# Gate sums moved to TensorE identity products, and the last low-part pass of two feed-forward slices issued as a row pair behind attention scores

## Chip, cores and metric

One Trainium2 chip, one core. The metric is device microseconds of one execution of the program; the time given is the median of several runs.

## The reference

Two parts in a row. The first is a recurrent attention (mLSTM) over 4 batches, 8 heads, 768 steps, head size 40:

```
m_new  = max(f[t] + m, i[t]);  f_stab = exp(f[t] + m - m_new);  i_stab = exp(i[t] - m_new)
C      = f_stab * C + i_stab * outer(v[t], k[t]);   n = f_stab * n + i_stab * k[t]
y[t]   = sigmoid(o[t]) * (C @ q[t]) / max(|n . q[t]|, 1)
```

The second is a feed-forward layer on the 3072 resulting rows of 320: `h = x @ w_in` (320 to 2048), `g = h * clip(h + 3, 0, 6) / 6`, `out = g @ w_out` (2048 to 320). All inputs and the output are float32.

## The kernel before

**Attention.** The time axis is cut into 6 chunks of 128 steps in each batch, so there are 24 chunks. Eight *units* of three chunks each are worked off in order; each unit has two *tasks*, one for each quad of four heads. For each task and chunk there is: `gate` (builds the 128x128 decay weights `gw` of four heads: from the chunk's cumulated log gates, by TensorE for the first seven, by a DMA broadcast `gw<-gsc` and a mask on GpSimd for the others, then four exponentials on ScalarE), `front` (state product L611, four score products q.k in pairs of 64-row halves L694, four products with the carried state L697, then VectorE multiplies scores by weights, L702, and from unit 2 on splits the result into three bfloat16 parts `p`), and `back` (weights times values, L742 or L744 to L747). `fin` normalises, applies the output gate, transposes (L799) and splits the result into `xh` and `xl`, the high and low float32r parts of the feed-forward's input. A front waits until the front before it has made its `p`.

**Gates.** `gates(c0, n)` works off `n` chunks of the gate sequences as [32, 128 n] tiles; `GP = [1, 2, 1, 2]` says how the six chunks are grouped. VectorE scans the running maximum `m_s`, forms the stabilised log forget gate `lf` and its cumulated sum `g_s` by chunk; GpSimd and VectorE form `i_s - m_s - g_s` (L458, L477); TensorE transposes that and `g_s` (L488, L490) into one PSUM bank; VectorE copies both out (`cT`, `gTs`; L492, L496), a product with `last` (L503) broadcasts the chunk's final sum, VectorE adds it to `cT` (L505), and ScalarE makes the exponentials `eG`, `wT` and `dec`.

**Feed-forward.** For each unit the 2048 hidden columns are 16 *slices* of 128. `mm1(u, f)` makes one slice of `h` for 384 rows: eight passes of 384 columns into one of two PSUM banks (`mm`): three for each of the two full 128-row blocks of the input (high.high, high.low, low.high), and two for the last 64 input rows. For those, `wtl` holds the high part of the weights in one half of the partitions and the low part in the other (the halves swap between even and odd slices), and the x tile holds its rows twice. So the seventh pass gives high.high plus low.high, and the eighth high.low plus low.low. Then ScalarE (L907) and VectorE (L909) make `g`, which frees the bank, and ScalarE and VectorE split it (L404, L917). `mm2(u, p)` takes a pair of slices: three row tiles, six products of 320 columns each (L936 to L938), accumulated over the unit in three further banks. Six `g` slots exist. `evac` copies the sums out and stores them.

**Order.** The order on every engine is made when the program is built, by a list planner (`Plan`): each step is a job with a due time and a list of events that it needs; the planner keeps a clock for each engine and picks the next request by readiness and due time. The program then runs in that order; an engine works its queue in order and waits for semaphores. The due times come from constants (`T0`, `SPAN` for a unit's place, `AH` for how far attention runs ahead, `MV` for the feed-forward, `BKO` for `back`, `FIN0` for the first unit's `fin`, `G0` to `G2` for gates, `STICK` for staying with attention). `ENGINES` gives for each kind of elementwise step the engine or the choice of engines. While TensorE has nothing to do before the feed-forward opens, `warm` puts 128-column products `pw` (L425) on it.

Of the kernel before, what the change touches and what calls it, by code (L numbers as in the profile page):

```python
# [46 lines left out]
SPAN = 70.624  # L47
T0 = 123.535
AH = 19.252
GP = [1, 2, 1, 2]  # L50
G0 = -120.578
G1 = -25.639
G2 = 24.583
AH1 = 73.471
FC = 0
FCS = {2: [[(0, 2)], [(0, 1), (1, 1)]], 3: [[(0, 3)], [(0, 2), (2, 1)], [(0, 1), (1, 1), (2, 1)], [(0, 1), (1, 2)]], 1: [[(0, 1)], [(0, 1)]]}
LON = -2.289
WAI = 24.113
WAO = -0.73
WAS = 84.596  # L60
MV = -25.163
DELTA = -1.445
EGW = 1
EV = 127.005
EG = 30.396
# [7 lines left out]
RATE = 3689.588  # L73
WN = 128
DELTA0 = 0.131
# [4 lines left out]
BL = 7.052  # L80
T_WARM = 6.9
WGAP = 0.055
ENGINES = 'dxpxadzddadddxddxxdaaaaxdapx'
BG = 1.587
BA = -0.13
BD = -0.329
GS = 6
FD = 2
FIN0 = -97.197
# [58 lines left out]
class Plan:  # L148
# [4 lines left out]
    def __init__(self, slots):  # L153
        self.free = {e: 0.5 for e in "padgq"}
        self.dma = 0.5
        self.slots = {k: [(At({}), i) for i in range(n)] for k, n in slots.items()}
        self.done = {}
        self.jobs = []
        self.waiting = {}
        self.fresh = []  # L160
        self.left = 0
        self.work = {}
        self.recent = []
        self.port = 0.0
        self.last = ""
        self.n = 0

    def add(self, due, gen, after=(), att=1, slack=None, hot=False):
        self.n += 1
        j = dict(due=due, n=self.n, gen=gen, t=At({}), eng=None, req=None, after=list(after), need=set(after), att=att, slack=DELTA if slack is None else slack, first=slack is not None, hot=hot)  # L170
# [91 lines left out]
    def run(self):  # L262
        self.settle()
        while self.jobs:
            best = {}
            for j in self.jobs:
# [20 lines left out]
                if e == "p" and self.last != "moe" and j["gen"].__name__ not in ("mm1", "mm2", "warm"):  # L287
                    due -= STICK
                k = (late, start if late else 0.0, due, j["n"])
# [8 lines left out]
            else:  # L298
                end = start + cost
                if e == "p":  # L300
                    kind = {"mm1": "moe", "mm2": "moe"}.get(j["gen"].__name__, j["gen"].__name__)
# [45 lines left out]
def mlstm_moe_kernel(ctx: ExitStack, tc: tile.TileContext, ig, fg, qkd, natd, ond, w_in, w_out, ident_d, out):  # L347
# [66 lines left out]
    def warm():  # L414
# [13 lines left out]
        f_s=[BH, S], i_s=[BH, S], m_s=[BH, S], lf=[BH, S], g_s=[128, S], last=[128, 128], gTs=[128, NC, BH], one=[BH, L], sel=[128, 8, L]).items()}  # L428
# [7 lines left out]
    def gates(c0, n):  # L436
        f_s, i_s, m_s, lf, g_s, last, gTs, mask, one = (GT[k] for k in ("f_s", "i_s", "m_s", "lf", "g_s", "last", "gTs", "mask", "one"))
# [16 lines left out]
        yield "d", ld(w)  # L454
        nc.vector.tensor_tensor_scan(m_s[:, a:z], f_s[:, a:z], i_s[:, a:z], m_s[:, a - 1 : a] if c0 else NEG, ALU.add, ALU.max)
        b, t = max(a, 1), plan.now["t"]
        e = yield psub(26, w)
        E(e).tensor_sub(i_s[:, a:z], i_s[:, a:z], m_s[:, a:z])  # L458
        ti, plan.now["t"] = plan.now["t"], t
# [4 lines left out]
        for c in cs:  # L464
            ks = slice(c * L, c * L + L)
            yield "d", ld(L)
# [8 lines left out]
        plan.now["t"] = later(t, ti)  # L475
        yield "d", ld(w)
        nc.vector.tensor_sub(i_s[:, a:z], i_s[:, a:z], g_s[:BH, a:z])  # L477
        yield "wait", "ident"
        if c0 == 0 and GB:
            yield "a", ca(128)  # L480
            nc.scalar.copy(GT["identb"], ident)
            event("identb")
        gs = yield ("get",) + banks(0, "o")
        pb = bank(gs, [128, 4, 4, BH], f"pc{c0}")
        pc, pg, pl = (pb[:, k, :n] for k in range(3))
        yield "p", mat(2 * n, 128, 1, 32, 32)
        for c in cs:
            nc.tensor.transpose(pc[:, c - c0, :], i_s[:, c * L : (c + 1) * L], ident[:BH, :BH])  # L488
        for c in cs:
            nc.tensor.transpose(pg[:, c - c0, :], g_s[:BH, c * L : (c + 1) * L], ident[:BH, :BH])  # L490
# [4 lines left out]
        yield "d", cd(32 * n)  # L495
        nc.vector.tensor_copy(gTs[:, hs], pg)  # L496
        yield "a", ca(32 * n)
        nc.scalar.activation(eG[:, hs], pg, AF.Exp)
        if c0 == 0:
            yield "d", cd(128)  # L500
            nc.vector.tensor_copy(last, ident[:, 127:128].broadcast_to([128, 128]))
        yield "p", mat(2, 32 * n, 2)
        nc.tensor.matmul(pl, last, gTs[:, hs], start=True, stop=True)  # L503
        yield "d", cd(32 * n)
        nc.vector.tensor_tensor(wT[:, hs], pl, cT[:, hs], ALU.add)  # L505
        yield "a", ca(32 * n)
        nc.scalar.activation(wT[:, hs], wT[:, hs], AF.Exp)
# [56 lines left out]
    def weigh(task):  # L564
# [4 lines left out]
        for cp in range(UNITS[task // 2]):  # L569
            _, _, _, c, r0 = where(task, cp)  # L570
            if c < NC - 1:
                yield "wait", f"wT{c}"
                e = yield pick(6, d=ld(168), g=cg(168), a=4 * ca(42))
# [99 lines left out]
    def front(task, cp):  # L673
# [21 lines left out]
        if cur is not None:  # L695
            for z, j, rows, hs in halves:
                nc.tensor.matmul(sp[:, z, 2 * L + j * E2 : 2 * L + j * E2 + E2], st[rows, 0, hs], cur[rows, j, :], start=True, stop=True)  # L697
        put(*sg)
# [115 lines left out]
    def weight_slice(kind, i, n):  # L814
# [22 lines left out]
        if kind == "i":  # L837
# [6 lines left out]
            e = yield pick(4, a=0.44, d=Lock(0.63))  # L844
# [33 lines left out]
    A = {}  # L878

    def mm1(u, f):  # L880
# [10 lines left out]
        yield "p", mat(8, NT)  # L891
        for n, (w, x) in enumerate(seq):
            nc.tensor.matmul(hp, w, x, start=n == 0, stop=n == len(seq) - 1)  # L893
        event(f"m1_{u}_{f}")
# [81 lines left out]
    for task in range(2 * NU):  # L976
# [18 lines left out]
        for cp in range(n):  # L995
# [15 lines left out]
            plan.add(due(u, k + cp), front(task, cp), [f"st{nm}", *last, *old] + ahead(rank[task, cp]), 1, sl)  # L1011
# [90 lines left out]
```

## Time and profile before

| | |
|---|---|
| median of 3 runs (lowest, highest) | 492.16 us (492.15, 494.31) |
| the profiled execution: time, span in the trace | 493.0 us, 491.3 us |
| TensorE busy / VectorE / ScalarE / GpSimd | 484.1 / 392.5 / 268.5 / 34.1 us |
| granted TensorE clock | 1.00 |
| first feed-forward product | 44.16 us after the span's start |

The busy time of TensorE counts records that overlap (a record's end is modelled), so a rate is read from the distance between two starts. "PEld" is the loading of weights, "x8" is the number of instructions in a row of a timeline; a float32 product is two instructions, a float32r or bfloat16 product one. A window's row gives, for each engine, the busy time and the number of instructions.

### The profile page before, as it was taken

What the parts mean: (1) busy time and instruction counts of PE and PEld (TensorE: products, weight loads), DVE (VectorE), ACT (ScalarE), POOL (GpSimd) and SP (SyncE); (2) the same over time, 40 slices, a digit from 0 to 9 for tenths busy, and PEclk for the clock granted to TensorE, in tenths of its full rate; (3) what the DMA queues carried; (4) which work ended last, traced back from release to release, by engine and by line L of the source; (5) the groups of instructions that cost most, each with busy time, mean ns of one, the idle gap of its engine ahead of it and who ended that gap; (6) DMA issues with size and microseconds to landing.
All of it is one profiled execution on the core that took longest, in us unless ns stands there. A gap on an engine that the chain in (4) does not pass through costs nothing.

```text
span 491.3 us, 10775 instructions
## 1 busy us (share of the span) xinstructions
PE 484.1 (99%) x4227; PEld 463.7 (94%) x4227; DVE 392.5 (80%) x926; ACT 268.5 (55%) x618; POOL 34.1 (7%) x55
## 2 busy tenths in 40 slices
PE   8999999999999999999999999999999999999997
PEld 8999898999999999999999999999999999999997
DVE  7999999988878898879799887889698798533332
ACT  4967969846344654556355644555355443434333
POOL 5001101001000101010010100010000100000000
PEclk9999999999999999999999999999999999999999
DMA  7678776323231514143142333242221210001001
GB/s 269 216 272 244 254 228 204 111 82 109 65 108 46 183 55 118 55 126 115 43 126 86 107 106 106 71 120 83 67 84 63 85 41 2 0 2 40 1 1 40
DMA packets 24626, 50.79 MB, mean 103 GB/s; under 512 B 2560, under 2 KB 9024, under 8 KB 24576
## 3 DMA queue, kind: packets, MB, share of 16 engines
q1 hardware_dynamic: 24576, 50.11, 31.7%
q8 instruction: 33, 0.54, 0.5%
q14 instruction: 17, 0.14, 0.1%
HBM read 46.07 MB, written 4.03 MB: 102 GB/s over the span
## 4 chain that ended last, share of the span: by engine, by line
PE 85%; DVE 6%; DMA 4%; ACT 2%; issue 1%; SPq 1%; POOL 0%; POOLq 0%; DVEq 0%; ACTq 0%
PE h L893 33%; PE acc L936 11%; PE acc L938 10%; PE acc L937 10%; PE s L694 5%; PE s L697 3%; PE s L611 2%; DMA nat<-in_nat_dram 2%; DMA gw<-gsc 2%; PE x L799 1%; PE pw L425 1%; PE o L744 1%; PE o L742 1%; PE o L746 1%; DMA st<-in_qk_dram 1%; PE gb L655 1%
## 5 line engine op out<-in xcount | busy, mean ns | idle before, releaser
L907 ACT ACTIVATE g<-h,half 128x384 f32<-128x384 f32 x128 | 73.6, 576 | 97.8 <-PE h L893 97.5
L936 PE MATMUL acc<-vh,gh 128*128 128x320 f32 x384 | 122.1, 318 | 0.0
L938 PE MATMUL acc<-vh,gl 128*128 128x320 f32 x384 | 118.9, 310 | 0.0
L937 PE MATMUL acc<-vl,gh 128*128 128x320 f32 x384 | 118.8, 309 | 0.0
L909 DVE SCALAR_TENSOR_TENSOR g<-g,h 128x384 f32<-128x384 f32 x128 | 70.3, 550 | 44.9 <-ACT g L907 44.6
L893 PE MATMUL h<-xh,whi 128*128 128x384 f32 x256 | 91.0, 355 | 2.3 <-DVE g L909 2.2
L404 ACT CAST gh<-g 128x384 fp32r<-128x384 f32 x128 | 65.2, 511 | 47.8 <-DVE g L909 47.3
L893 PE MATMUL h<-xh,wlo 128*128 128x384 f32 x256 | 86.6, 338 | 0.0
L893 PE MATMUL h<-xl,whi 128*128 128x384 f32 x256 | 86.4, 338 | 0.0
L917 DVE TENSOR_TENSOR gl<-g,gh 128x384 fp32r<-128x384 f32 x128 | 73.9, 579 | 9.6 <-ACT gh L404 8.0
L936 PEld LDWEIGHTS acc<-vh,gh 128*128 128x128 f32 x384 | 72.1, 188 | 1.3
L937 PEld LDWEIGHTS acc<-vl,gh 128*128 128x128 f32 x384 | 72.2, 188 | 0.0
L938 PEld LDWEIGHTS acc<-vh,gl 128*128 128x128 f32 x384 | 72.1, 188 | 0.0
L667 ACT ACTIVATE gw<-gw,cT 128x128 f32<-128x128 f32 x164 | 54.2, 392 | 29.7 <-POOL gw L661 29.4
L893 PEld LDWEIGHTS h<-xh,whi 128*128 128x128 f32 x256 | 48.0, 188 | 6.2 <-DVE g L909 5.0
L661 POOL TENSOR_SCALAR_AFFINE_SELECT gw<-gw 128x512 f32<-128x512 f32 x41 | 27.9, 680 | 352.6 <-DMA gw<-gsc 208.4
L893 PEld LDWEIGHTS h<-xl,whi 128*128 128x128 f32 x256 | 48.2, 188 | 0.0
L893 PEld LDWEIGHTS h<-xh,wlo 128*128 128x128 f32 x256 | 48.1, 188 | 0.0
L893 PE MATMUL h<-xh,wtl 128*128 128x384 f32 x128 | 43.3, 338 | 0.0
L893 PE MATMUL h<-xl,wtl 128*128 128x384 f32 x128 | 43.2, 337 | 0.0
L702 DVE TENSOR_TENSOR gw<-s,gw 128x512 f32<-128x512 f32 x48 | 32.9, 685 | 6.3 <-PE s L697 5.3
L694 PE MATMUL s<-st 64*128 64x128 f32 x384 | 34.3, 297 | 0.3 <-DMA st<-in_qk_dram 0.3
(105 smaller groups left out, 754.2 us busy)
## 6 DMA issues: line engine op xcount, KB each, us to landing
st<-in_qk_dram SPq DMA_DIRECT2D x48, 256.0 KB, 3.1
gw<-gsc SPq DMA_DIRECT2D x41, 256.0 KB, 3.2
nat<-in_nat_dram SPq DMA_DIRECT2D x16, 492.0 KB, 4.4
rawi<-in_w_in_dram SPq DMA_DIRECT2D x8, 640.0 KB, 4.7
rawo<-in_w_out_dram SPq DMA_DIRECT2D x8, 640.0 KB, 4.9
on<-in_on_dram SPq DMA_DIRECT2D x8, 480.0 KB, 3.8
out_dram<-ob SPq DMA_DIRECT2D x24, 160.0 KB, 1.8
f_s<-in_fg_dram SPq DMA_DIRECT2D x1, 96.0 KB, 2.1
```

Of the source, the lines that this page charges most:

```text
L404: nc.scalar.copy(dst, src)
L661: nc.gpsimd.affine_select(gw, gw, pattern=[[0, 4], [1, L]], compare_op=ALU.is_ge, fill=NEG, base=0, channel_multiplier=-1)
L667: nc.scalar.activation(gw[:, h, :], src[:, h, :], AF.Exp, bias=cT[:, c, r0 + h : r0 + h + 1], scale=1.0)
L694: nc.tensor.matmul(sp[:, z, hs], st[rows, 1, hs], st[rows, 0, hs], start=True, stop=True)
L702: nc.vector.tensor_tensor(gw.rearrange("p (z j) l -> p z (j l)", z=2), sp[:, :, : 2 * L], gw.rearrange("p (z j) l -> p z (j l)", z=2), ALU ...
L893: nc.tensor.matmul(hp, w, x, start=n == 0, stop=n == len(seq) - 1)
L907: nc.scalar.activation(g, hp, AF.Relu, bias=half, scale=1.0 / 6.0)
L909: nc.vector.scalar_tensor_tensor(g, g, 1.0, hp, ALU.min, ALU.mult)
L917: E(e).tensor_sub(gl, g, gh.bitcast(F32))
L936: nc.tensor.matmul(acc, gh[:, ts_], VH[f // 4][:, f % 4, :], start=f == 0, stop=False)
L937: nc.tensor.matmul(acc, gh[:, ts_], VL[p][:, f % 2, :], start=False, stop=False)
L938: nc.tensor.matmul(acc, gl[:, ts_], VH[f // 4][:, f % 4, :], start=False, stop=f == NF - 1)
```

## The change

- `gates`: the subtractions of `m_s` and `g_s` from `i_s`, the copy `gTs`, the tile `last`, its product and the sum for `wT` are gone from GpSimd and VectorE. Each of four small matrices of a chunk is now accumulated in PSUM by products of the [32, 128] gate tiles with a 32x32 identity or its negative (`neg`, made by one ScalarE instruction): `cT` from three products, the exponent of `wT` from four, `g_s` transposed from one, the broadcast of the chunk's last sum from one. `GP` becomes `[1, 1, 1, 3]`.
- `mm1` of the units 1 to 6: seven passes; the eighth is left to a new job `tail(u, i)` for the slices 2i and 2i+1. An open tail is issued by the next `front`, directly behind its score and state products: two products on 64 rows each, one in each half of the array, with the high part of the weights alone (low.low is dropped there). If no front comes first, the planner issues the tail by itself as two full 128-row passes. Both banks stay taken until then.
- The planner holds back fronts of the units 2 to 7 while no tail is open (`HOLD`), and prefers them while one is (`HOLD` and the pair's cost).
- `mm2` of the units 1 to 7 gets a later due time (`M2`).
- Most planner constants change, and `ENGINES` at some places: the second cast in the split of `p` (index 18) goes from VectorE to ScalarE, the subtractions of index 23 from a choice of VectorE and GpSimd to VectorE alone; index 1 goes to VectorE alone, index 7 and 12 to a choice of VectorE and GpSimd.

```diff
-BKO = 5.044
+TP = 1
+M2 = 7.748
+HOLD = 10.039
+TAIL = -13.256
+WT = 0.096
+BKO = -68.995
-STICK = 49.917
+STICK = 40.018
-SPAN = 70.624
-T0 = 123.535
-AH = 19.252
-GP = [1, 2, 1, 2]
+SPAN = 66.836
+T0 = 169.071
+AH = 16.371
+GP = [1, 1, 1, 3]
-MV = -25.163
+MV = -7.655
-ENGINES = 'dxpxadzddadddxddxxdaaaaxdapx'
+ENGINES = 'ddpxadzxdaddxxddxxaaaaaddaxx'
-FIN0 = -97.197
+FIN0 = -277.025
...
+                if e == "p" and self.open and name == "front":
+                    due -= HOLD
+                    cost = cost + self.open[0][1]
+                elif j["hold"]:
+                    due += HOLD
...
-        e = yield psub(26, w)
-        E(e).tensor_sub(i_s[:, a:z], i_s[:, a:z], m_s[:, a:z])
-        yield "d", ld(w)
-        nc.vector.tensor_sub(i_s[:, a:z], i_s[:, a:z], g_s[:BH, a:z])
-        for c in cs:
-            nc.tensor.transpose(pc[:, c - c0, :], i_s[:, c * L : (c + 1) * L], ident[:BH, :BH])
-        for c in cs:
-            nc.tensor.transpose(pg[:, c - c0, :], g_s[:BH, c * L : (c + 1) * L], ident[:BH, :BH])
+        parts = {0: ((i_s, eye), (m_s, neg), (g_s, neg)), 1: ((i_s, eye), (m_s, neg), (g_s, neg), (None, eye)), 2: ((g_s, eye),), 3: ((None, eye),)}
+        for ks, count in (((0,), 6), ((2, 1, 3), 12)):
+            yield "p", mat(count * n, 32, 2, 32, 64)
+            for k in ks:
+                for c in cs:
+                    for m, (src, rhs) in enumerate(parts[k]):
+                        lhs = src[:BH, c * L : (c + 1) * L] if src is not None else g_s[:BH, (c + 1) * L - 1 : (c + 1) * L].broadcast_to([BH, L])
+                        nc.tensor.matmul(pb[:, k, c - c0, :], lhs, rhs, start=m == 0, stop=m == len(parts[k]) - 1)
-        nc.vector.tensor_copy(gTs[:, hs], pg)
-            nc.vector.tensor_copy(last, ident[:, 127:128].broadcast_to([128, 128]))
-        nc.tensor.matmul(pl, last, gTs[:, hs], start=True, stop=True)
-        nc.vector.tensor_tensor(wT[:, hs], pl, cT[:, hs], ALU.add)
-        nc.scalar.activation(wT[:, hs], wT[:, hs], AF.Exp)
+        nc.scalar.activation(wT[:, hs], pw, AF.Exp)
...
+        if plan.open:
+            (um, i, job), _ = plan.open.pop()
+            plan.jobs.remove(job)
+            for z in range(2):
+                f = 2 * i + z
+                nc.tensor.matmul(HQ[um, f], wtl[z * HR : z * HR + HR, f * 128 : f * 128 + 128], XT[um][1][z * HR : z * HR + HR, 2, :], start=False, stop=True)
+            event(f"tail{um}_{i}")
...
+    def tail(u, i):
+        cost = mat(2, UNITS[u] * L)
+        plan.open.append(((u, i, plan.now), mat(1, UNITS[u] * L)))
+        plan.now["t"] += WT
+        yield "p", cost, TAIL
+        plan.open.pop()
+        for f in (2 * i, 2 * i + 1):
+            nc.tensor.matmul(HQ[u, f], wtl[:, f * 128 : f * 128 + 128], XT[u][1][:, 2, :], start=False, stop=True)
+        event(f"tail{u}_{i}")
...
+        if TP <= u < NU - 1:
+            yield "p", mat(7, NT)
+            for n, (w, x) in enumerate(seq[:7]):
+                nc.tensor.matmul(hp, w, x, start=n == 0, stop=False)
+            HQ[u, f] = hp
+            event(f"m1_{u}_{f}")
+            yield "wait", f"tail{u}_{f // 2}"
...
+            if f % 2 and TP <= u < NU - 1:
+                plan.add(moe_at(u, f / NF) - MV, tail(u, f // 2), [f"m1_{u}_{f}"], 0)
-            plan.add(moe_at(u, (2 * p + 2) / NF) - MV, mm2(u, p), pre + [f"g{u}_{2*p}", f"g{u}_{2*p+1}", f"ws{p}" if u >= NV else f"wo{p}"], 0)
+            plan.add(moe_at(u, (2 * p + 2 + (M2 if u >= TP else 0.0)) / NF) - MV, mm2(u, p), pre + [f"g{u}_{2*p}", f"g{u}_{2*p+1}", f"ws{p}" if u >= NV else f"wo{p}"], 0)
```

More of the change, by code (lines that the diff above doesn't have):

```diff
@@ L72 @@
 COLDX = 1.9
-RATE = 3689.588
+RATE = 4000
 WN = 128
-DELTA0 = 0.131
+DELTA0 = 0.24
 HOPP = 0.254
@@ L300, in run @@
                 if e == "p":
-                    kind = {"mm1": "moe", "mm2": "moe"}.get(j["gen"].__name__, j["gen"].__name__)
+                    kind = {"mm1": "moe", "mm2": "moe", "tail": "moe"}.get(j["gen"].__name__, j["gen"].__name__)
                     if kind != self.last:
@@ L427, in mlstm_moe_kernel @@
     GT = {k: early["ea"].tile(sh, F32, name=k) for k, sh in dict(
-        f_s=[BH, S], i_s=[BH, S], m_s=[BH, S], lf=[BH, S], g_s=[128, S], last=[128, 128], gTs=[128, NC, BH], one=[BH, L], sel=[128, 8, L]).items()}
+        f_s=[BH, S], i_s=[BH, S], m_s=[BH, S], lf=[BH, S], g_s=[128, S], neg=[BH, BH], one=[BH, L], sel=[128, 8, L]).items()}
     GT.update({k: early["ea"].tile([128, L], BF16, name=k) for k in ("mask", "identb")})
@@ L436, in gates @@
     def gates(c0, n):
-        f_s, i_s, m_s, lf, g_s, last, gTs, mask, one = (GT[k] for k in ("f_s", "i_s", "m_s", "lf", "g_s", "last", "gTs", "mask", "one"))
+        f_s, i_s, m_s, lf, g_s, neg, mask, one = (GT[k] for k in ("f_s", "i_s", "m_s", "lf", "g_s", "neg", "mask", "one"))
         if c0 == 0:
```

91 lines of the change are left out of this document (50 added, 41 removed).

## The prediction, made before the changed kernel ran

> **What bounds the kernel now.** I read the page's engine totals first, then the chain that ended last, then busy time by stage, the waits, and the timeline of TensorE for the distances between starts.
>
> ```profile
> PE 484.1 (99%) x4227; PEld 463.7 (94%) x4227; DVE 392.5 (80%) x926; ACT 268.5 (55%) x618; POOL 34.1 (7%) x55
> ...
> PE 85%; DVE 6%; DMA 4%; ACT 2%; issue 1%; SPq 1%; POOL 0%; POOLq 0%; DVEq 0%; ACTq 0%
> ```
>
> TensorE is taken for nearly the whole span and carries 85% of the chain. By stage:
>
> ```profile
> 20.00:44.16 24.16, 24.10 (x314) 22.49 (x310) 23.80 (x63) 18.13 (x48) 1.58 (x2) 1.00 0.69 213
> 44.16:100.00 55.84, 53.55 (x392) 50.81 (x393) 52.56 (x117) 45.40 (x99) 4.44 (x6) 1.00 0.64 207
> 100.00:411.00 311.00, 310.58 (x2825) 297.79 (x2824) 265.41 (x625) 161.20 (x372) 21.85 (x33) 1.00 0.28 89
> 411.00:491.30 80.30, 77.19 (x490) 75.34 (x488) 34.57 (x69) 30.98 (x61) 0.00 (x0) 1.00 0.04 13
> ```
>
> Columns: window, length, then busy time of PE, PEld, DVE, ACT and POOL, the granted clock, the DMA share. Four stages. Up to 44.16 us no feed-forward runs; VectorE is full (23.80 of 24.16) and TensorE's busy time is partly filler. From 44 to 100 both are nearly full. From 100 to 411 TensorE is busy for 310.58 of 311 us, the granted clock is 1.00, and VectorE has 46 us free: there only TensorE's work counts. From 411 only feed-forward is left. TensorE hardly waits at all after the start:
>
> ```profile
> PE h L893 <- DVE g L909: 2.2, 4, 0.8
> ...
> PEld h L893 <- DVE g L909: 5.0, 11, 1.1
> ```
>
> (engine, line, releaser: us in total, times, longest). These are the same waits seen by the product and by its weight load, for a PSUM bank that VectorE has not yet read; the four long ones lie before 100 us. So the end is the start of the feed-forward plus TensorE's work behind it, and at most some 5 us of waits are left to remove. An instruction taken from TensorE after 44 us moves the end by its own issue time.
>
> **The tails: what a pair saves.** The pace of a full pass from the chain in order of time, the shapes behind it from TensorE's timeline:
>
> ```profile
> 203.02 1.41 PE h L893 x8
> ...
> 208.47 0.34 PE L893 MATMUL h<-xl,wtl 128*128 128x384 f32 x1
> ...
> 209.44 0.72 PE L694 MATMUL s<-st 64*128 64x128 f32 x8
> 209.99 0.54 PE L697 MATMUL s<-C,st 64*128 64x42 f32 x8
> 210.46 0.45 PE L893 MATMUL h<-xh,whi 128*128 128x384 f32 x1
> 210.74 0.34 PE L893 MATMUL h<-xl,whi 128*128 128x384 f32 x1
> ```
>
> Eight passes of 384 columns are 1.41 us of the chain, 0.176 each, although the record of one says 0.34. Two eighth passes are 0.35 us. Do two 64-row products run beside each other? Full-height products of the same columns and kind, for comparison:
>
> ```profile
> 22.86 1.05 PE L655 MATMUL gb<-g_s,sel 128*128 128x128 f32 x8
> 23.75 0.98 PE L742 MATMUL o<-nat,gw 128*128 128x42 f32 x8
> ```
>
> Eight L655 take 0.89 us, 0.111 each; eight L694 on alternating halves take 0.55, 0.069 each, with the change of shape in it. So halves overlap. A tail pair costs at the least one more pair at L697's rate (0.47 us for 8, so 0.118), at the most two passes behind one another (0.35). I take one pass, 0.176, because the pair streams the same 384 columns once through both halves and stands in a place where the array is already in halves. The step back to full height, 0.28 instead of 0.176 at 210.46, is paid once, as today. A pair then saves 0.175 us; ends 0 and 0.233.
>
> How many pairs? Units 1 to 6 have 48 tails; the fronts of the units 2 to 7 are 36, and a front takes one. The rest go out as two full passes, which costs what it cost. Held fronts wait for a tail, and a tail is offered 0.096 us after its slices, so a front that is ready goes first. I take 32 pairs, since some fronts will wait for their decay weights or the `p` before. Ends: 18 (half) and 36. The sum is 32 x 0.175 = 5.6 us saved, ends 0 and 8.4.
>
> **What the tails can cost.** Both `mm` banks are now held until the tail. Then ScalarE and VectorE must read one before the next slice can begin:
>
> ```profile
> 208.91 0.58 ACT L907 ACTIVATE g<-h,half 128x384 f32<-128x384 f32 x1 [1.87 <-PE h L893]
> ...
> 209.52 0.55 DVE L909 SCALAR_TENSOR_TENSOR g<-g,h 128x384 f32<-128x384 f32 x1 [1.54 <-ACT g L907]
> ...
> L406 DVE CAST p<-gw 128x512 bf16<-128x512 f32 x72 | 30.9, 430 | 0.6
> L404 ACT CAST vb<-nat 128x504 bf16<-128x504 f32 x24 | 14.6, 608 | 2.1 <-DVE nat L597 1.1 <-DMA nat<-in_nat_dram 0.9
> ```
>
> The pass that began at 208.47 has left TensorE at 208.65; ScalarE starts 0.26 later, takes 0.58, VectorE follows after 0.03 and takes 0.55. With a hand-over back like the first, 1.7 us. What hides it are the second products of an earlier pair:
>
> ```profile
> 212.50 0.39 PE L936 MATMUL acc<-vh,gh 128*128 128x320 f32 x1
> 212.74 0.31 PE L937 MATMUL acc<-vl,gh 128*128 128x320 f32 x1
> 212.88 0.31 PE L938 MATMUL acc<-vh,gl 128*128 128x320 f32 x1
> ```
>
> at 0.146 each, 18 a pair: 2.64 us. That is why `M2` puts them a pair later, and the six `g` slots hold three pairs. Cost 0; if the cover is gone, up to 1.7 us for each of 48 pairs. In the last unit the postponed products fill the end, where TensorE has nothing else, so they cost nothing.
>
> The first two rows also show what a separate visit to attention costs: 0.24 instead of 0.146 at its end (212.50 to 212.74). Now a back often stands beside a front; with `BKO` 74 us earlier and fronts held, some backs will go alone. I take 8 more visits at 0.1 us, +0.8; ends 0 and +2.5 (25 visits).
>
> **Casts.** The second cast of 36 `p` goes from VectorE (0.43, above) to ScalarE (about 0.6, from the cast of 504 columns above). ScalarE is busy for 161 of 311 us, VectorE gets 15 us back, and neither is the bound there: 0. Were ScalarE late, L907 behind it would be, and through it the `mm` banks. The other moved choices concern 8 weight slices each, at most 0.8 us an instruction, in the full stretch before 100 us; I take 0 for them and for the 2.2 to 5.0 us of waits there a gain of 0.5, ends 0 and 3.
>
> **Gates: VectorE's side.**
>
> ```profile
> L477 DVE TENSOR_TENSOR i_s<-i_s,g_s 32x128 f32<-32x128 f32 (+1 forms) x4 | 1.3, 325 | 0.0
> ...
> L505 DVE TENSOR_TENSOR wT<-pc,cT 128x32 f32<-128x32 f32 (+1 forms) x4 | 0.8, 194 | 0.2
> L496 DVE COPY gTs<-pc 128x32 f32<-128x32 f32 (+1 forms) x4 | 0.7, 179 | 0.0
> ...
> L501 DVE COPY last<-ident 128x128 f32<-128x128 f32 x1 | 0.5, 468 | 0.0
> ```
>
> These 13 instructions go: 3.3 us by their records. Records on VectorE overlap:
>
> ```profile
> 7.28 0.17 DVE L492 COPY cT<-pc 128x32 f32<-128x32 f32 x1
> 7.38 0.41 DVE L467 TENSOR_TENSOR_SCAN g_s<-one,lf 32x128 f32<-32x128 f32 x1
> ```
>
> a copy of 0.17 is followed 0.10 later. At 0.07 to 0.08 less for each of 13 it is 2.3 us of VectorE's time, in the stage where VectorE is full. If VectorE alone set the start of the feed-forward, it would come 2.3 us earlier.
>
> **Gates: TensorE's side.** Added are 9 products a chunk, 54 in all, 108 instructions, in place of 12 transposes and 8 instructions of L503. The nearest rows:
>
> ```profile
> 14.39 0.39 PE L503 MATMUL pc<-gTs,last 128*128 128x32 f32 x2
> 14.62 0.50 PE L425 MATMUL pw<-ones 128*128 128x128 bf16 x6
> 15.10 0.31 PE L488 MATMUL pc<-ident,i_s 32*128 32x32 f32 x2
> 15.25 0.28 PE L490 MATMUL pc<-ident,g_s 32*128 32x32 f32 x2
> ```
>
> L488 has the very shape, but is a transpose: 0.075 each. Float32 products with 128 columns of weights are 0.111 (L655, above) and 0.115 (L503: 0.23 for 2). I take 0.113, because kind decides more than height, as these rows show:
>
> ```profile
> L742 PEld LDWEIGHTS o<-nat,gw 128*128 128x128 f32 x96 | 11.8, 191 | 0.3
> L799 PEld LDWEIGHTS x<-ident,on 128*128 128x128 f32 x72 | 9.2, 141 | 1.1 <-PE h L893 0.7
> ...
> L488 PEld LDWEIGHTS pc<-ident,i_s 32*128 32x128 f32 x6 | 0.7, 136 | 0.5 <-DVE ht L406 0.2
> ```
>
> Loading weights for a transpose takes 136 ns on 32 rows and 141 on 128, for a product 191. So 108 x 0.113 = 12.2, less 12 x 0.075 and 8 x 0.115, is 10.4 us more; at the transpose's rate 6.3. [...]
>
> The cover is the filler:
>
> ```profile
> 6.90:20.00 13.10, 4.21 (x55) 3.26 (x53) 1.00 0.85 312
> 20.00:44.16 24.16, 5.82 (x89) 5.29 (x89) 1.00 0.69 213
> ...
> 36.68 3.24 PE L425 MATMUL pw<-ones 128*128 128x128 bf16 x55
> 39.76 1.04 PE L742 MATMUL o<-nat,gw 128*128 128x42 f32 x8
> ```
>
> (the first two: filler alone.) 55 of them take 3.08 us, 0.056 each, so 144 are 8.1 us, 3.1 of them before 20 us, where the gates are. So TensorE's own work before the feed-forward grows by 10.4 against 8.1 us of cover: at that price the start would be 2.3 us later, at the lower price not at all. Between 2.3 earlier by VectorE and 2.3 later by TensorE I take 0. The lower end is -2.3, the upper +5: the early surplus is 10.4 - 3.1 = 7.3 us, and fronts, `p` and weight slices behind it on VectorE's queue may take back only part of it. GpSimd loses L458; nothing waits for it. ScalarE gains one small instruction.
>
> **The sum.** -5.6 (tails) + 0.8 (visits) - 0.5 (waits) + 0 (gates) = -5.3 us. From the profiled execution, 493.0, that gives 487.7; it lies 0.84 above the median, so 486.9 on the median's scale.
>
> **The rivals.**
> (a) *TensorE becomes the bound before 44 us.* Tails as forecast, the feed-forward starts 4 us later: 492.16 - 5.3 + 4 = 490.9, no measurable change. For it: 7.3 us of early surplus; against it: 5.0 us of later filler. Chance 0.17.
> (b) *The change does not do what it says*: the halves do not overlap for 384 columns, or few fronts meet an open tail. Then the tails give 0 and the rest +0.3: 492.5. Against it: L694's 0.069 against 0.111. Chance 0.09.
> (c) *Slower: the held banks.* Each tail is followed by an emptied pair of banks, and if VectorE has a 0.7 us scores or `p` instruction in hand, L909 comes that much later than the 1.7 us. It decides once TensorE idles more than 5.6 / 48 = 0.12 us a pair; at 0.3 us a pair it is +14.4, so 492.16 - 5.3 + 14.4 = 501.3, and at 0.2, 496.5. For it: VectorE is 85% busy from 100 to 411 us and the waits that exist are for just this release. Against it: 2.64 us of cover for 1.7. [...] Chance 0.12.
> (d) *Better:* VectorE's 2.3 us and 2 us of the waits before 100 us come on top: 492.16 - 5.3 - 3.8 = 483. Chance 0.12.
> The forecast itself: 0.50, from 484.5 to 489.5.
>
> **How the numbers follow.** A measurement of this kernel can tell about 0.5%, 2.5 us, from no change: faster means below 489.7. Faster is nearly all of the forecast and (d), and a quarter of (a): 0.66. Same is most of (a), most of (b), a little of the forecast: 0.21. Slower is (c) and a part of (b): 0.13. The range for 8 in 10 goes from 482.0, which takes in (d), to 494.0, which takes in (a) and (b) and leaves (c) out.
>
> **What would show it.** Right: TensorE's timeline has about 32 pairs of 64-row products of 384 columns behind L697, each adding about 0.18 us before the next full-height product; L893's full passes fall from 1024 to about 928 plus 16 x 2 unpaired tails; the first feed-forward product starts between 42 and 46 us; the wait of `h` for `g` stays below 5 us. Wrong: a pair adding 0.3 us or more; far fewer pairs; a wait of `h` for `g` of tens of times 0.2 us between 100 and 411 us; a start of the feed-forward at 48 us.

## The result and the profile after

The changed kernel takes 517.13 us (median of 4 runs, 512.3 to 518.21), the kernel before beside it 492.68 us (492.15 to 494.31): a ratio of 1.0471, 95% interval 1.0399 to 1.0544. The forecast was 486.9, faster.

The engine totals and the line of the granted clock of the page (40 slices of 12.9 us), then the shares of the chain that ended last:

```profile
PE 508.3 (99%) x4284; PEld 486.9 (95%) x4284; DVE 372.2 (72%) x863; ACT 280.8 (55%) x647; POOL 43.3 (8%) x67
...
PEclk8568969999999999999999999999999999999999
...
PE 94%; DMA 3%; ACT 1%; DVE 0%; POOL 0%; issue 0%; POOLq 0%; DVEq 0%; ACTq 0%
```

TensorE is still taken all the time, and carries 94% of the chain instead of 85%. What is new is the second line, the clock in tenths of full speed (9 is 0.9 or more): 9 in every slice before, it is now 5 to 8 in five of the first six. By stretch (columns as before: window, length, PE, PEld, DVE, ACT, POOL, clock, DMA share, GB/s):

```profile
5.90:8.60 2.70, 2.70 (x31) 2.66 (x30) 1.17 (x4) 1.26 (x4) 0.00 (x0) 1.00 1.01 395
8.60:43.20 34.60, 34.60 (x217) 32.12 (x214) 14.62 (x35) 12.97 (x43) 1.92 (x2) 0.56 0.40 135
43.20:68.70 25.50, 23.96 (x293) 22.36 (x292) 20.83 (x53) 16.14 (x43) 3.82 (x5) 0.96 0.64 209
68.70:77.00 8.30, 8.30 (x40) 8.13 (x40) 5.74 (x14) 3.17 (x5) 0.63 (x1) 0.50 0.70 172
100.00:411.00 311.00, 310.49 (x2737) 295.74 (x2737) 251.94 (x584) 184.89 (x424) 27.59 (x41) 1.00 0.31 97
```

The same stretch of the kernel before:

```profile
8.60:43.20 34.60, 34.31 (x436) 31.61 (x436) 33.89 (x101) 27.78 (x81) 2.86 (x4) 1.00 0.73 248
```

In these 34.6 us TensorE began 436 instructions before and 217 after, at a clock of 0.56, and VectorE's busy time fell from 33.89 to 14.62 us: the engine that was full there now waits. The timeline of TensorE shows both ends of it:

```profile
5.89 0.40 PE L508 MATMUL pc<-ident,i_s 32*128 32x32 f32 x2
6.13 0.38 PE L508 MATMUL pc<-neg,m_s 32*128 32x32 f32 x2
6.36 0.38 PE L508 MATMUL pc<-neg,g_s 32*128 32x32 f32 x2
...
12.94 0.61 PE L508 MATMUL pc<-neg,m_s 32*128 32x32 f32 x2
13.36 0.61 PE L508 MATMUL pc<-neg,g_s 32*128 32x32 f32 x2
...
68.73 0.67 PE L932 MATMUL h<-xh,whi 128*128 128x384 f32 x1
69.19 0.52 PE L932 MATMUL h<-xl,whi 128*128 128x384 f32 x1
69.51 0.52 PE L932 MATMUL h<-xh,wlo 128*128 128x384 f32 x1
```

A gate product (two instructions) takes 0.23 us from start to start at 6.13, and 0.42 at 12.94. The first feed-forward product starts at 68.73 us instead of 44.16, and its passes follow each other at 0.32 us instead of 0.176. After 77 us the clock stays at 1.00.

The clock falls three times: at about 8.8 us, at about 29.3, after it had been at 1.00 from 25.9 on, and at about 66.9, after it had been at 1.00 from 43.0 on. The last gate product starts at 33.6, so the last fall is not beside these products; it comes 2 us behind a wait of TensorE of 1.54 us:

```profile
64.97 0.55 PE L819 MATMUL x<-ident,on 128*128 128x128 f32 x3 [1.54 <-DVE xl L825]
```

The first and the last feed-forward product before, and the last one after:

```profile
44.16 0.44 PE L893 MATMUL h<-xh,whi 128*128 128x384 f32 x1
487.88 0.31 PE L938 MATMUL acc<-vh,gl 128*128 128x320 f32 x1
```

```profile
511.24 0.31 PE L977 MATMUL acc<-vh,gl 128*128 128x320 f32 x1
```

So the account is: start 24.6 us later; from there to the start of the last product 442.5 us (68.73 to 511.24) instead of 443.7 (44.16 to 487.88); together 23.4, and the span is 23.3 longer. About half of the 8.3 us from 68.7 to 77 are the clock's as well (the last fall; 0.50 in the row above). The rest of the body is therefore some 5 us shorter than before.

The tails, in the timeline behind a front's scores, and all instructions of the two lines (times in ns, minimum/median/maximum, then the first and the last start):

```profile
127.90 0.54 PE L710 MATMUL s<-C,st 64*128 64x42 f32 x8
128.27 0.42 PE L716 MATMUL h<-xl,wtl 64*128 64x384 f32 x2
128.62 0.42 PE L975 MATMUL acc<-vh,gh 128*128 128x320 f32 x1
128.88 0.31 PE L976 MATMUL acc<-vl,gh 128*128 128x320 f32 x1
```

```profile
L716 PE MATMUL h<-xl,wtl x36: 413/418/420, 128.3 to 425.8; 64*128 64x384 f32 x36
```

```profile
L908 PE MATMUL h<-xl,wtl x60: 337/337/428, 143.9 to 459.7; 128*128 128x384 f32 x60
```

18 pairs in halves and 30 tails sent out as two full passes. From L710 to the first full step behind it are 0.37 + 0.35 + 0.26 = 0.98 us. Without a tail the same place is 0.47 + 0.24 to 0.28, about 0.73. So a pair adds 0.25 us and saves 0.10 of the 0.35 that two passes take.

### The profile page after: what moved, and what is told of

The parts are those of the page before. It is cut to its first block, busy times and chain, and to the rows that moved or that the text cites. A ratio compares the mean times of both kernels' runs of the same rounds, so it can differ in the third digit from the quotient of the medians.

```text
span 514.6 us, 10916 instructions
## 1 busy us (share of the span) xinstructions
PE 508.3 (99%) x4284; PEld 486.9 (95%) x4284; DVE 372.2 (72%) x863; ACT 280.8 (55%) x647; POOL 43.3 (8%) x67
## 4 chain that ended last, share of the span: by engine, by line
PE 94%; DMA 3%; ACT 1%; DVE 0%; POOL 0%; issue 0%; POOLq 0%; DVEq 0%; ACTq 0%
PE h L925 23%; PE acc L975 11%; PE acc L976 11%; PE acc L977 11%; PE h L932 9%; PE s L707 6%; PE pc L508 4%; PE s L710 3%; PE s L624 2%; PE o L762 2%; PE pw L437 2%; PE h L908 2%; DMA gw<-gsc 2%; PE gb L668 2%; PE x L819 2%; PE o L764 1%
## 5 line engine op out<-in xcount | busy, mean ns | idle before, releaser
L946 ACT ACTIVATE g<-h,half 128x384 f32<-128x384 f32 x128 | 68.8, 576 | 59.8 <-PE h L932 28.9
L948 DVE SCALAR_TENSOR_TENSOR g<-g,h 128x384 f32<-128x384 f32 x128 | 67.0, 550 | 35.3 <-ACT g L946 34.7
L956 DVE TENSOR_TENSOR gl<-g,gh 128x384 fp32r<-128x384 f32 x126 | 69.3, 567 | 2.8 <-ACT gh L416 2.2
L416 ACT CAST gh<-g 128x384 fp32r<-128x384 f32 x128 | 63.1, 513 | 13.6 <-DVE g L948 12.8
L925 PE MATMUL h<-xh,whi 128*128 128x384 f32 x192 | 67.7, 352 | 0.0
L925 PE MATMUL h<-xh,wlo 128*128 128x384 f32 x192 | 64.9, 338 | 0.0
L925 PE MATMUL h<-xl,whi 128*128 128x384 f32 x192 | 64.8, 338 | 0.0
L744 DVE TENSOR_TENSOR p<-gw,p 128x512 bf16<-128x512 f32 x36 | 25.0, 695 | 16.7 <-ACT p L416 16.7
L925 PEld LDWEIGHTS h<-xh,whi 128*128 128x128 f32 x192 | 36.0, 188 | 0.9
L925 PEld LDWEIGHTS h<-xl,whi 128*128 128x128 f32 x192 | 36.1, 188 | 0.0
L925 PEld LDWEIGHTS h<-xh,wlo 128*128 128x128 f32 x192 | 36.1, 188 | 0.0
L925 PE MATMUL h<-xh,wtl 128*128 128x384 f32 x96 | 32.5, 338 | 0.0
```

The lines of the kernel that those rows point to most:

```text
L416: nc.scalar.copy(dst, src)
L925: nc.tensor.matmul(hp, w, x, start=n == 0, stop=False)
L946: nc.scalar.activation(g, hp, AF.Relu, bias=half, scale=1.0 / 6.0)
L948: nc.vector.scalar_tensor_tensor(g, g, 1.0, hp, ALU.min, ALU.mult)
L956: E(e).tensor_sub(gl, g, gh.bitcast(F32))
```

## The experiments

Theories after the result. **Theory 1:** the new gate products keep so little of TensorE's array at work that its clock is taken down, and most of what it does from 8.8 to 43 us runs at half speed (0.56 on the mean); the rest of the change is near what was forecast. It has two forms: what counts is the share of time in which columns stream (**1a**), or the rows that a product uses count as well (**1b**). Theory 2 is that the products' own time moves the start, theory 3 that the held banks or the later second products cost the time. Rivals: the planner's price for these products (64 columns of weights where the trace has loads of 32x128), which packs the stage wrongly; the order made by the changed constants; the tails' held banks; the casts on ScalarE. Ratios are to the kernel before on the same chip, with 95% intervals.

**The gates taken back (e1_old_gates).** The changed kernel with the old `gates`, its tiles and `GP = [1, 2, 1, 2]`.

> The changed kernel with the gates of before (their code and GP = [1, 2, 1, 2]); tails, held fronts, casts and all other constants as changed. Theory 1 (the gates' small products let the granted clock fall to half from about 8.7 us on, and everything on TensorE up to 43 us takes twice as long): granted clock 1.00 throughout, first feed-forward product at 43 to 47 us, time 486 to 490 us, since the body behind it stays. Theory 2 (the products' own time on TensorE, 108 at 0.11 us, moves the start): the same here. Theory 3 (the held banks or the later second products cost the time): stays above 505 us.

500.98 us, 1.0142 (1.0118 to 1.0166). The clock is 1.00 up to 92 us and the feed-forward starts at 43.65: theory 1 holds for the start. But the time is not the forecast's. The first unit takes 69.5 us here, 56.9 before:

```profile
64.00:92.00 28.00, 23.55 (x182) 21.80 (x181) 26.14 (x61) 20.98 (x45) 2.51 (x4) 1.00 0.63 205
92.00:106.00 14.00, 9.45 (x87) 8.30 (x86) 13.51 (x28) 11.05 (x22) 0.64 (x1) 0.76 0.47 147
```

TensorE idles 4.5 us in each of these two windows while VectorE is nearly full, and the longest waits of the feed-forward's second products are for split weights (`PE acc L974 <- ACT vh L416`, 3.8 us). Behind the first of these windows, at 1.00, the clock is 0.76 in the second. The new constants and engine choices, in the order that the planner makes of them, thus cost something of their own. The late start hides it in the changed kernel, whose list of waits has none of a second product for split weights.

**The gates alone (e2_new_gates_alone).** The kernel before with the new `gates` and its tiles.

> The kernel before with the new gates code alone (GP = [1, 2, 1, 2], all constants as before, no tails). Theory 1: the clock falls to about 0.5 somewhere between 8 and 45 us, the first feed-forward product comes 15 to 25 us later than 44.16, time 507 to 518 us. Theory 2: the clock stays at 1.00 and the start comes 5 to 10 us later, 497 to 502 us. Theory 3: no change, 492 us.

515.32 us, 1.0435 (1.0379 to 1.049). The clock is down without any tail or new constant, and the feed-forward starts at 65.6:

```profile
8.00:16.00 8.00, 8.00 (x65) 7.69 (x64) 2.98 (x9) 2.33 (x9) 0.00 (x0) 0.75 0.85 334
16.00:36.00 20.00, 20.00 (x127) 19.08 (x127) 9.32 (x25) 9.00 (x27) 0.00 (x0) 0.50 0.23 75
36.00:48.00 12.00, 12.00 (x146) 10.89 (x144) 11.56 (x30) 8.32 (x24) 0.00 (x0) 1.00 0.65 217
```

TensorE is busy for 20.00 of 20.00 us from 16 to 36 us, and the clock is 0.50 all the same: here "busy" by the records does not go with a full clock.

**The true price in the planner (e3_true_price).**

```diff
-            yield "p", mat(count * n, 32, 2, 32, 64)
+            yield "p", mat(count * n, 32, 2, 32, 128)
```

> The changed kernel with one number changed: the planner charges the gates' products 0.111 us each, as measured at full clock, instead of 0.057, and so puts more filler between them (274 fillers before the feed-forward instead of 169). Theory 1: the clock stays at 1.00 in nearly all of the first 45 us; the start comes at 52 to 58 us (10 us more of products and 5 us more of filler than before), time 495 to 502 us. Theory 2: the fillers are only more work, and the start is later than the 68.7 us of the changed kernel, above 517 us.

Four executions took 510.05 to 521.37 us; for the two shorter ones (510.05 and 516.12) the ratio is 1.0383 (1.0307 to 1.046). The planner lays 274 fillers instead of 169, and the clock stands at 0.51 from 16 to 43 us nonetheless. So the price is not the cause, and theory 1's expectation is missed as well: with the added fillers between the blocks of gate products the fall only comes later (0.95 from 8 to 16 us, where the changed kernel has 0.55).

**Fillers behind every gate product (e4_fill, e5_fill_same_shape).** Three 128-column fillers behind each of the 54 products, first on full height, then on the products' own 32 rows.

```diff
+                        for _ in range(3):
+                            nc.tensor.matmul(FILL["pw"][:, :WN], ones[:, :128], ones[:, :WN], start=True, stop=True)
```

```diff
+                        for _ in range(3):
+                            nc.tensor.matmul(FILL["pw"][:, :WN], ones[:BH, :128], ones[:BH, :WN], start=True, stop=True)
```

> The changed kernel in its own order, with three filler products (128 columns, 0.056 us each at full clock) put behind each of the 54 gate products: 162 instructions, 9.1 us of added TensorE work, nothing taken away. Theory 1: the clock holds at 1.00 in the first 45 us, so the start comes EARLIER than the 68.7 us of the changed kernel, at 52 to 60 us, and the time falls to 500 to 510 us. Theory 2: the start comes 9 us later, 78 us, time 526 us.

> The run before (three fillers behind each gate product) had fillers of full height between products on 32 rows; each change of shape cost about 0.1 us and the clock fell all the same. [...] Theory 1a (the clock follows the share of time in which columns stream, whatever the rows): clock 1.00 up to 45 us, start of the feed-forward at 55 to 63 us, time 500 to 508 us. Theory 1b (rows count as well): the clock falls to 0.5 from about 9 us on, start later than 85 us, above 530 us.

e4: 544.62 us, 1.1021 (1.0945 to 1.1098), start 97.01; e5: 526.89 us, 1.066 (1.0624 to 1.0696), start 81.42. In both the clock falls (0.58 from 8 to 24 us in e4, 0.50 from 8.60 to 32.00 in e5), so what theory 1 said of e4 is missed; e5 is nearer to 1b (81.42 against more than 85) than to 1a (55 to 63). The timelines of TensorE ahead of the fall, of e4 and then of e5:

```profile
7.18 0.40 PE L511 MATMUL pc<-neg,m_s 32*128 32x32 f32 x2
7.52 0.34 PE L513 MATMUL pw<-ones 128*128 128x128 bf16 x3
7.79 0.40 PE L511 MATMUL pc<-neg,g_s 32*128 32x32 f32 x2
```

```profile
6.22 0.35 PE L511 MATMUL pc<-neg,m_s 32*128 32x32 f32 x2
6.41 0.33 PE L513 MATMUL pw<-ones 32*128 32x128 bf16 x3
6.58 0.35 PE L511 MATMUL pc<-neg,g_s 32*128 32x32 f32 x2
```

A group is 0.61 us with full-height fillers and 0.36 with fillers of 32 rows, so each of the two changes of height in a group costs about 0.12, an estimate from the difference of 0.25. In e4 the fillers' own 0.17 us (three at 0.056) are thus only about a quarter of a group. e5 has no such change, its fillers are nearly half of a group, and it is still at half clock:

```profile
8.60:32.00 23.40, 23.40 (x161) 21.40 (x161) 7.27 (x19) 5.26 (x22) 0.47 (x1) 0.50 0.36 128
```

What is left for it is the rows (1b).

**The same products on 128 rows (e6_tall_fill, e7_tall, e13_tall_fill_one).** `i_s`, `m_s`, `neg` on 128 rows (`g_s` has them already), of which 32 to 127 are zero, with three, no, and one filler behind each product. The sums are unchanged.

```diff
-                        lhs = src[:BH, c * L : (c + 1) * L] if src is not None else ...
+                        lhs = src[:, c * L : (c + 1) * L] if src is not None else ...
-        eye = ident[:BH, :BH]
+        eye = ident[:, :BH]
```

> [...] Theories 1a and 1b: clock 1.00 up to 45 us, start at 55 to 63 us although 162 fillers are added to the changed kernel, time 500 to 508 us. Theory 2 (the products' own time, not the clock): start later than 75 us, above 525 us.

> The changed kernel with its gate products on all 128 rows (zeros in the added ones), no fillers added: the same instructions and the same order, 32 columns in each 0.11 us, 12% of streaming. Theory 1a: the clock falls as in the changed kernel, start near 68 us, 517 us. Theory 1b: four times the rows may hold it; then start at 50 to 56 us, 495 to 502 us.

> As the run with gate products on 128 rows and three fillers each, with one filler instead: 54 fillers, 3.0 us, instead of 162 and 9.1 us. A product and its filler take 0.28 us. If the clock holds, the start comes 6 us before the 62.1 us of that run, at 56 us, so the products' own time is about 9 us of the 24.6 us and the clock the rest; time 499 to 503 us. If it does not hold (as without fillers, 57.3 us), the start lies at 58 us or later and part of the clock is lost for a while.

e6: 507.26 us, 1.0268 (1.0239 to 1.0296). Order and number of instructions are those of the changed kernel plus 162 fillers. The timeline of TensorE, then the stretches:

```profile
8.18 0.36 PE L514 MATMUL pc<-ident,g_s 128*128 128x32 f32 x2
8.38 0.33 PE L516 MATMUL pw<-ones 128*128 128x128 bf16 x3
8.54 0.36 PE L514 MATMUL pc<-ident,g_s 128*128 128x32 f32 x2
```

```profile
8.60:43.20 34.60, 33.85 (x440) 32.34 (x438) 19.86 (x50) 17.55 (x56) 1.92 (x2) 1.00 0.53 179
43.20:62.00 18.80, 16.77 (x219) 15.45 (x218) 16.26 (x40) 11.80 (x31) 3.48 (x5) 1.00 0.59 202
```

A group takes 0.36 us as in e5, with the same columns. On TensorE only the rows differ, and the clock is 1.00 instead of 0.50. By the filler's pace (128 columns in 0.056 us) the 448 columns of a group take 0.20 of the 0.36 us in both, an estimate; so the share that streams cannot tell them apart. This is the pair of runs that decides for 1b. The start is 62.08.

e7, without fillers: 505.21 us, 1.0221 (1.0187 to 1.0255), start 57.25. By the same pace the 32 columns of an instruction are 0.014 us, 12% of the 0.115 measured in the changed kernel.

```profile
5.40:21.40 16.00, 15.68 (x163) 15.29 (x159) 9.78 (x24) 8.10 (x28) 2.62 (x5) 1.00 0.76 261
21.40:32.00 10.60, 10.60 (x75) 9.84 (x75) 6.86 (x16) 5.06 (x14) 1.45 (x1) 0.52 0.50 173
```

The clock falls, from 1.00 to 0.52, behind an unbroken run of 4.6 us of 32-column products (16.8 to 21.4); the start lies just above what 1b said (50 to 56). One filler each (e13): 503.11 us, 1.0184 (1.0139 to 1.023), start 58.29, clock 1.00 to 40 us and at half from about 41 to 44 (0.50 from 42 to 44). So of the 4.7%, 2.0 (e6) to 2.9 (e13) are gone, although these runs carry fillers of their own, 9.1 and 3.0 us. An estimate without them: e6's 507.26 less 9.1 is 498.2 us, 0.8% above before, so that close to 4 of the 4.7% are the clock's. No run has the changed kernel at full clock without added fillers.

**The tails alone (e8_tails_alone, e9_no_tails_control).** Before's constants and gates, with the new tails, `M2`, `HOLD`, `TAIL`, `WT`; the control has `TP = 99`, so that no unit has a tail or a later `M2`.

> The kernel before with the tails alone: gates, due times, casts and all other constants as before, plus TP, M2, HOLD, TAIL and WT of the change. The planner makes 10 pairs and 38 tails by themselves. Theory 1: tails are harmless and nearly worthless: each pair takes 0.25 us where two passes took 0.35, so 10 x 0.10 = 1 us faster, 491 to 493 us, no measurable change; the wait of the first for the second VectorE step stays below 5 us. Theory 3 (held banks and later second products cost time): above 497 us, with waits of the slices for g.

> The control to the tails alone: its code and constants with the tails switched off (TP = 99), so all slices have eight passes and the second products keep their due times. Theory 1 (the 0.5% of the tails alone comes from the tails): the same as before, 0.998 to 1.002 of it. Rival 4 (it comes from the slightly other order in the first 45 us that the code's new charges make): 0.993 to 0.996 of before, as the tails alone.

e8: 491.57 us, 0.9945 (0.9926 to 0.9964), with 10 pairs and 38 tails alone; start 43.95. The control: 495.95 us, 1.0044 (1.0028 to 1.006), which neither theory expected: something in the code's new charges costs 0.4% without any tail. e8 and, below, e15 are the only versions faster than both kernels. In e8 the seven-pass slices (L924) have no wait for a bank in the list; the one that is there belongs to the eight-pass slices of the units 0 and 7:

```profile
PE h L931 <- DVE g L947: 1.4, 2, 0.8
```

**Without the second products' delay (e10_tails_no_delay, e11_same_order_full_passes).** e10 is e8 with `M2 = 0.0`; e11 is e10 with every pair sent out as two full passes at the same place.

```diff
-            for z in range(2):
-                f = 2 * i + z
-                nc.tensor.matmul(HQ[um, f], wtl[z * HR : z * HR + HR, f * 128 : f * 128 + 128], XT[um][1][z * HR : z * HR + HR, 2, :], start=False, stop=True)
+            for f in (2 * i, 2 * i + 1):
+                nc.tensor.matmul(HQ[um, f], wtl[:, f * 128 : f * 128 + 128], XT[um][1][:, 2, :], start=False, stop=True)
```

> The tails alone with M2 = 0: the second products keep the due times of before; the planner makes 20 pairs instead of 10. Theory 1 (a pair saves 0.10 us, an open pair of banks is covered): 20 x 0.10 = 2 us less than the control, 0.995 to 0.997 of before. Theory 3 (without the delay the cover of the emptied banks is gone): waits of the slices for g grow above 10 us, 500 us or more.

> The run above in the very same order, but each of its 20 pairs is issued as two full-height passes in the same place. Theory 1: a pair takes 0.25 us and two passes 0.35, so this is 20 x 0.10 = 2 us slower than the run above, 0.4%. The sum of the prediction (0.176 for a pair) says 3.5 us slower. Rival 4 (pairs are worth nothing): no difference.

e10: 525.72 us, 1.0669 (1.0632 to 1.0706); e11: 529.68 us, 1.0729 (1.0702 to 1.0756). In e10:

```profile
PE h L924 <- DVE g L947: 23.9, 15, 3.7
```

```profile
300.00:400.00 100.00, 89.08 (x746) 83.28 (x746) 67.00 (x158) 41.29 (x97) 5.71 (x9) 0.93 0.25 74
```

This is rival (c) of the prediction, called up by taking its cover away: TensorE idles for 11 of 100 us, waiting for the two banks, and the clock falls to 0.93 with it. From e8 to e10 the ratio grows by 7.2%, some 36 us, of which the 23.9 us of waits are the part that is shown; e10 has 20 pairs and another order, so this is the delay's worth in this order, not a price by itself. The pair against two full passes in the same order: 1.0669 to 1.0729, 4.0 us between the medians for 20 pairs, about 0.2 each, with an uncertainty of the same size as the difference. In e11's timeline, where a `back` follows:

```profile
157.03 0.54 PE L709 MATMUL s<-C,st 64*128 64x42 f32 x8
157.50 0.62 PE L714 MATMUL h<-xl,wtl 128*128 128x384 f32 x2
157.96 0.21 PE L762 MATMUL o<-vb,p 128*128 128x84 bf16 x1
```

From L709 to the next product are 0.93 us; in e10 the same place is 0.37 + 0.36 = 0.73. There a pair saves 0.20, twice of what it saves ahead of second products: in the places where these follow, the same distance to the first full step is 0.97 in e10 and 1.08 in e11, which confirms the 0.10.

**The delay alone (e15_delay_alone).** e9 with `M2` at its 7.748 in the units 1 to 7, no tails.

> The control without tails, with the later due time of the second products (M2) for the units 1 to 7. If the delay carries the gain of the tails alone, 0.994 to 0.998 of before, and the waits that the control has between 100 and 500 us are gone; if the tails carry it, 1.002 to 1.006, as the control.

492.07 us, 0.9972 (0.9954 to 0.9989). Against the control's 1.0044 it is 0.7% less, without a tail. With the tails (e8) it is 0.3% less again, but there the intervals overlap: the larger part of e8's gain over the control is the delay's. What the delay saves is only in part seen: TensorE's products wait 1.6 us between 100 and 500 us in the control and not at all in e15.

**More pairs (e14_more_pairs).** e8 with `HOLD = 30`, `TAIL = 10`: 18 pairs.

> The tails alone with HOLD = 30 and TAIL = 10: the planner makes 18 pairs and 30 single tails instead of 10 and 38. By 0.10 us a pair it is 0.8 us faster than the tails alone: 0.991 to 0.994 of before. If the later fronts or longer held banks cost more than that: 0.996 to 1.005, with waits of the slices for g.

497.84 us, 1.009 (1.0056 to 1.0124), slower than either forecast. Eight more pairs than e8, and 6.3 us more. The waits of `h` for `g` are 5.2 us in total (3.6 of a seven-pass slice, 1.6 of the others) against 1.4, which explains 3.8; the rest was not taken apart.

**The cast on ScalarE (e12_cast_on_scalar).** The kernel before with the second cast of `p` on ScalarE.

```diff
-ENGINES = 'dxpxadzddadddxddxxdaaaaxdapx'
+ENGINES = 'dxpxadzddadddxddxxaaaaaxdapx'
```

> The kernel before with one letter of ENGINES changed: the second cast of p (index 18) on ScalarE instead of VectorE, 36 casts of 0.43 us. The prediction had 0 for it: 0.998 to 1.003 of before. If VectorE's load carries the waits that are left, 1 to 2 us faster; if ScalarE becomes late for the slices, slower by 1 us or more, with waits of the slices for g.

497.73 us, 1.008 (1.0057 to 1.0103).

```profile
PE h L893 <- DVE g L909: 4.5, 6, 1.5
```

This wait was 2.2 us before, which explains 2.3 us. The cast costs 4 us, with the order that the planner makes of it.

## Why the prediction was wrong

**The step that failed: "Gates: TensorE's side", by the cover.** The price of an instruction was right (0.113 forecast, 0.115 measured in the rows at 6.13 and 6.36), and so the 10.4 us of added work. Two things behind it were wrong.

*The filler was counted as cover.* 144 fillers of 0.056 us were to give way. The groups of L425 before and of L437 after:

```profile
L425 PE MATMUL pw<-ones 128*128 128x128 bf16 x200 | 15.9, 242 | 1.1 <-POOL ones L418 1.1
```

```profile
L437 PE MATMUL pw<-ones 128*128 128x128 bf16 x169 | 15.4, 267 | 1.1 <-POOL ones L430 1.1
```

169 stand where 200 stood, so 31 gave way, 1.7 us. Worked out: 10.4 - 1.7 = 8.7 us should be left at full clock. e6 bears it out: its start of 62.08, less its own 162 fillers at 0.056 (9.1), is 53.0, an estimate of the changed kernel's start at full clock, which is 8.8 us after 44.16. That the two agree so closely is partly luck: TensorE idles 2.8 us in e6 between 8.60 and 62.00. The early surplus of 7.3 us, of which only "+5" went into the upper end, was not taken back.

*The clock was taken as given.* It stood at 1.00 in every window of before, and I carried it over without asking what held it there. The filler had a part in that, as e13 (one behind each product: 1.00 to 40 us) against e7 (none: 0.52 from 21.4 to 32.0) suggests, and I treated it as free room. From 53.0 (that estimate) to the measured 68.73 are 15.7 us: the clock's share of the 24.6, of which the last fall has about 0.9 (half of 66.9 to 68.73). What brought the last fall about is not shown; there is the wait of 1.54 us ahead of it, and in e1 and e10 a lower clock goes with idle stretches as well (0.76 with 4.5 of 14 us idle, 0.93 with 11 of 100). Two things already there could have raised the question: much of TensorE's busy time in that stage was filler on full height, and the planner's own `mat` weighs a product's work by its rows (`m.w = count * cols * passes * rows / 128.0`) and counts everything as `COLDX` = 1.9 times as long when that work falls below `COLS` in a window (`warm_at`, `stream`), while the new products use 32 of 128 rows. These are charges of the program; no run here measures them.

In windows of 0.5 us from 0 to 99 us the trace of the changed kernel shows a clock of 1.00 in 113, of 0.50 in 79, and something between in the six where it changes. TensorE's records fill the whole 34.60 us from 8.60 on, and the fall comes some 2.9 us after the first gate product (5.89 to about 8.8). In e5 a TensorE that was busy for 23.40 of 23.40 us was at 0.50 with its gate products and fillers on 32 rows; in e6, with the same on 128 rows, it was at 1.00.

**VectorE's side** (2.3 us sooner if VectorE alone set the start) never counted. VectorE was no longer what the stage waits for; one of its waits is on the gate products themselves:

```profile
DVE cT L513 <- PE pc L508: 18.7, 4, 9.4
```

**The tails' saving** was mis-sized: 32 pairs at 0.175 = 5.6 us were forecast, 18 at 0.10 = 1.8 were there in the changed kernel, all 18 with second products behind them. The number lies at the lower end I gave (18), the saving between its ends of 0 and 0.233. The halves do run beside each other (0.25 us against 0.35 for two passes), but a pair ahead of second products takes these 0.25 us and not the one pass of 0.176 that I chose. "A front that is ready goes first" was the assumption for 32, and 30 tails found none.

**The extra visits** (+0.8): from 100 to 411 us TensorE turns from feed-forward to attention 58 times before and 59 after. One visit instead of eight, +0.1.

**The held banks** at 0 with `M2` was right, and its mechanism too: without the delay the seven-pass slices wait 23.9 us for a bank (e10), with it not at all, in e8 as in the changed kernel, where the products of `h` have no wait for `g` in the list and the weight loads of the eight-pass slices 0.5 us (`PEld h L932 <- DVE g L948`). Rival (c) did not occur; the slower end came from elsewhere, which no rival of mine held. Rival (a) named the right place and stopped at 4 us.

**Casts and constants** at 0, with 0.5 of gain, were wrong: e12 puts the cast at +4 us, and e1 against e8 (old gates and tails in both) puts all new constants and engine choices at about 2%, 10 us, where the start is early. In the changed kernel this doesn't show, probably since the weights are long split when a feed-forward begins at 68.73. That neither engine "is the bound there" was read from shares of busy time, although the prediction itself names ScalarE's L907 as the way by which a bank comes free.

The some 5 us by which the rest of the body is shorter can be divided at the first product of unit 1, before and after:

```profile
101.07 0.34 PE L893 MATMUL h<-xh,whi 128*128 128x384 f32 x1
```

```profile
123.91 0.34 PE L925 MATMUL h<-xh,whi 128*128 128x384 f32 x1
```

18 second products, 2.6 us, stand behind this border after that stood ahead of it before. With them put back, the stretch ahead of it is 55.2 + 2.6 - 4.1 (half of the 8.3 us at half clock) = 53.7 us instead of 56.9, and the stretch behind it 387.3 - 2.6 = 384.7 instead of 386.8 (both to the start of the last product). So some 3 us fall to the first unit, where no tail is, and 2.1 to the rest, near the 1.8 of the tails; this is an estimate. What stays open is what the later start, the delay and the other new constants each have in it.

## What to carry to other kernels

Filler that an engine runs while it waits for others is not free room: ask what goes with it, here the clock (e13 with one filler behind each product 1.00 to 40 us, e7 with none 0.52 from 21.4 to 32.0), and what of the new work can stand in the same place. Price a matrix product twice: by its issue time, and by the granted clock that is seen beside it; here 108 small instructions on 32 rows took 0.115 us each at first, and the clock was 0.56 from 8.60 to 43.20 us. Where work is postponed to hide a wait, try the postponing alone: here it gave more (0.7%) than the change that it was to serve added to it (0.3%).

## What the hardware showed that I had not expected

- The same groups of one gate product (two instructions of 32 columns) and three fillers, 0.36 us a group at full clock, had a granted clock of 0.50 on 32 rows (e5, 8.60 to 32.00 us) and of 1.00 on 128 rows (e6, 8.60 to 43.20 us), although 96 of these rows hold zeros. The filler of both is zero too.
- On full height, 32-column products without filler had 1.00 only for a time: the clock fell after an unbroken 4.6 us of them (e7, 0.52 from 21.4 to 32.0).
- A change of height between products cost about 0.12 us, an estimate: 0.61 us a group against 0.36 (e4, e5), with two changes in a group.
- Two 64-row products of 384 columns cost 0.25 us ahead of second products, against 0.176 for one full-height pass and 0.35 for two.
